# TensorE's program in a loop of two rounds, the first of which only jumps past it

## The chip, the core and the metric

The kernel runs on one core of one Trainium2 chip. The core has five engines with instruction streams of their own: TensorE (PE, matmuls; PEld is its loading of weights), VectorE (DVE), ScalarE (ACT), GpSimd (POOL) and SyncE (SP, which here only issues transfers), and 16 DMA engines that share the work of all DMA queues. The metric is the device time of one execution in microseconds (us).

## What is computed

One decoding step: one row `x` of 512 values, 32 heads, 8192 cached keys and values of 128 for each head, then a gate from a small GLU. All numbers are float32.

```python
def _A_ref(x, k_cache, v_cache, wq, wo):        # H, Dh = 32, 128; k_cache, v_cache: (1, 32, 8192, 128)
    q = (x @ wq).reshape(B, Sq, H, Dh).transpose(0, 2, 1, 3)
    scores = einsum("bhqd,bhkd->bhqk", q, k_cache) * (Dh ** -0.5)
    p = softmax(scores, axis=-1)
    o = einsum("bhqk,bhkd->bhqd", p, v_cache)
    return o.transpose(0, 2, 1, 3).reshape(B, Sq, H * Dh) @ wo

def _B_ref(x, w_gate, w_up, w_down):            # F = 1376
    return (sigmoid(x @ w_gate) * (x @ w_up)) @ w_down

xn = layernorm(x)
out = x + _A_ref(xn, ...) * silu(_B_ref(xn, ...))
```

Keys and values are 268 MB of the 294 MB that are read.

## The kernel before

All synchronisation is written out by hand with semaphores; nothing is scheduled by a planner. Each engine runs its own list of instructions in the order in which the program text calls that engine.

Heads are taken in 16 pairs (`NP`). One pair's keys are 8 MB, laid out as 128 partitions of 16384 numbers: head 2i in the upper 64 partitions, head 2i+1 in the lower. There are three such buffers: `slots[0]` and `slots[1]` take the keys by turns, `slots[2]` the values (and before them `wq`, after them the weights of the GLU). The last pair's values go to `slots[0]`, and `wo` to `slots[1]`.

*Prologue.* SP issues the loads of `wq` and of the first two pairs' keys; ACT those of `x`. Layer norm follows on DVE, PE and ACT (L179-L198), then q = xn @ wq on PE (L206) and its spreading over the partitions (L218).

*Pairs.* For pair i, DVE multiplies the keys by q (L281) and sums over the 128 numbers of each key (L282), which gives the scores; L284 takes their maximum per partition. PE turns these maxima into a row (L246), DVE reduces the row to two numbers (L276), PE spreads them (L248), ACT forms the exponentials (L296), PE sums them (L250). When the pair's values are there, 32 matmul lines weigh them (L255), ACT copies the sums (L301), PE gathers them (L260), DVE divides (L288, L289) and ACT places the result by two small transfers.

*Loads.* SP issues, one behind the other, the keys of pair i, when pair i-2's sums have been taken (L282), and the values of pair i-1, when L255 of pair i-2 has ended and so left `slots[2]` (L312-L314). Its queue is in order: a wait for the one holds up the other.

*TensorE's program.* All engines but PE have their pairs unrolled. PE's first 15 pairs are a loop (L265), since its instructions are the same for each; waits inside it are by `taken` (L240), which waits for a semaphore and takes the counted value away again. `head_slot={PE.engine: 0}` has the loop's first instruction loaded at the first slot of an instruction-fetch block, so padding stands ahead of it. The last pair stands behind the loop (L269), since its values are in another buffer; then come the matmuls of the GLU (L356, L384), the folds (L377) and those with `wo` (L402, L406). In PE's stream each matmul line of the program, in float32, is two weight loads and two matmuls.

Of the kernel before, what the change touches and what calls it, by code (L numbers as in the profile page):

```python
# [12 lines left out]

P = 128
EPS = 1e-5


@with_exitstack
def kernel(
# [12 lines left out]
    nc = tc.nc  # L32
# [6 lines left out]
    NP = H // 2  # L39
# [17 lines left out]

    W_ENDS, W_FOLD = (14, 24, 28, 30, 31, 32), 28

    PE, DVE, ACT, SP, POOL = nc.tensor, nc.vector, nc.scalar, nc.sync, nc.gpsimd  # L60

# [5 lines left out]
    def sb(name, *shape):  # L69
        return nc.alloc_sbuf_tensor(name, [P, *shape], F32)[:]  # L70
# [10 lines left out]
    slots = [sb(f"slot{i}", SLOT) for i in range(3)]  # L81
# [27 lines left out]
    def semaphore(name):  # L109
        sems.append(nc.alloc_semaphore(name))  # L110
        return sems[-1]


    class Steps:
        def __init__(self, name):
            self.sem, self.n = semaphore(name), 0
# [9 lines left out]
    def load(eng, name, dst, src, *after):  # L126
        wait(eng, *after)
        if name not in loads:
            loads[name] = [semaphore(f"s_{name}"), 0]
        loads[name][1] += 16  # L130
        eng.dma_start(dst, src).then_inc(loads[name][0], 16)  # L131
        return loads[name][0], loads[name][1]

    def wait(eng, *steps):
        for s in steps:
            if s is not None:
                eng.wait_ge(*s)
# [4 lines left out]
    s_val = semaphore("s_val")  # L142
# [27 lines left out]
    ld_xr = load(ACT, "xr", x_row[0:P:GP, :], xv.rearrange("(g c) -> g c", g=NG), c_xrow)  # L170
    c_eps = dve(DVE.memset(eps_t, EPS))
    c_id = pool(POOL.memset(ident, 0.0))
# [29 lines left out]
    for k in range(KT):  # L202
        for b in range(NQ // NG):
            for g in range(NG):
                c = (b * NG + g) * QT
                ins = PE.matmul(big[b][g * GP:g * GP + 1, :], xn[:, k:k + 1], wq_t[:, k, c:c + QT],  # L206
                                start=(k == 0), stop=(k == KT - 1))
# [32 lines left out]
    def taken(sem, n):  # L240
        PE.wait_ge(sem, n)
        PE.nop().then_inc(sem, -n)  # L242

    def pair(v, loaded):
        taken(maxed, 1)
        PE.matmul(pt[0:1, :], mx[:, 0:1], ident, start=True, stop=True).then_inc(turned, 1)  # L246
        taken(reduced, 1)
        PE.matmul(pm, ones[:1, :], mx[:1, 1:3], start=True, stop=True).then_inc(spread_m, 1)  # L248
        taken(powers, 2)
        PE.matmul(pn[:, Dh:], half, rs, start=True, stop=True)  # L250
        loaded()

        for j in range(0, NB, HT):
            g = j // HT % NG
            ins = PE.matmul(po[g * GP:g * GP + 2 * HT, :], weights[:, j // HT, :], v[:, j * Dh:(j + HT) * Dh],  # L255
                            start=(j < HT * NG), stop=(j >= NB - HT * NG))
        ins.then_inc(valued, 1)
        taken(copied, 1)
        for b in range(HT):
            ins = PE.matmul(pn[:, :Dh], pick[:, b:2 * HT:HT], o1[:, b * Dh:(b + 1) * Dh],  # L260
                            start=(b == 0), stop=(b == HT - 1))
        ins.then_inc(picked, 1)

    wait(PE, c_pick, c_id)
    with nc.Fori(0, NP - 1, engines=OrderedEngineSet([PE.engine]), head_slot={PE.engine: 0}):  # L265
        pair(slots[2], lambda: taken(s_val, 16))

    v_last = semaphore("s_v_last")
    pair(slots[NP % 2], lambda: PE.wait_ge(v_last, 16))  # L269


    summed, outs, placed = {}, {}, {}
# [78 lines left out]
    for dst, src, ld in ((big[0], wg_t, ld_g), (big[1], wu_t, ld_u)):  # L351
        wait(PE, ld)
        for c0, f0, w, g1 in ((0, 0, FW, 0), (FW, F - P, GP, g0)):
            for k in range(KT):
                for g in range(g1, NG):
                    ins = PE.matmul(dst[g * GP:g * GP + 1, c0:c0 + w], xn[:, k:k + 1],  # L356
                                    src[:, k, f0 + g * w:f0 + (g + 1) * w], start=(k == 0), stop=(k == KT - 1))
# [24 lines left out]
    for c in range(FP + 1):  # L382
        g = c % NG * GP
        ins = PE.matmul(big[0][g:g + 1, :], hid[:, c, 0:1], wd_t[:, c, :] if c < FP else wd_last,  # L384
                        start=(c < NG), stop=(c + NG > FP))
# [11 lines left out]
    for ld, r1 in zip(ld_o, W_ENDS):  # L397
        wait(PE, ld)
        for r in range(r0, r1):
            if r < W_FOLD:  # L400
                g = r % NG * GP
                ins = PE.matmul(big[0][g:g + 1, :], o_all[:, r:r + 1], wo_t[:, r, :],  # L402
                                start=(r < NG), stop=(r + NG >= W_FOLD))
                continue
            for g in range(NG):
                ins = PE.matmul(acc[g * GP:g * GP + 1, :], o_all[:, r:r + 1], wo_t[:, r, g * GC:(g + 1) * GC],  # L406
                                start=(r == W_FOLD), stop=(r == WR - 1))
# [8 lines left out]
    t = dve(DVE.tensor_mul(g_row, g_row, acc))  # L416
    wait(DVE, t)
    t = dve(DVE.tensor_add(g_row, g_row, x_row))  # L418
    SP.wait_ge(s_out, 16)
    SP.nop().then_inc(s_out, -16)  # L420
    wait(SP, t)
# [36 lines left out]
```

## Time and profile before

| | |
|---|---|
| time, median of 3 runs (lowest to highest) | 687.58 us (687.45 to 687.75) |
| profiled execution: span from its first to its last instruction | 685.6 us |
| instructions in the profile | 3694 |
| read from memory | 293.74 MB, 428 GB/s over the span |
| mean granted TensorE clock | 0.664 |

The profile is of one execution, and gives its span but no other time of it. Its page has, among other parts, the busy time of each engine; the span in 40 equal slices with a digit for the busy tenths of each; the DMA queues with packets, megabytes and the share of 16 engines' span that their packets took; and the chain of work that ended last, followed back from the last instruction. Queue q1 is SP's, q10 ACT's; queues of the kind "instruction" carry the engines' own programs. A timeline row is: start, duration, engine, line, operation, out<-in, partitions x elements, count, and in brackets the idle time before it and what ended that. "PEq" is PE's sequencer, which works through waits and jumps.

### The profile page before, as it was taken

The page shows a single profiled execution, that of the slowest core. Times are in us where ns is not written, and L with a number is a line of the kernel's source. Part 1 is how long each engine was busy: PE and PEld are TensorE (multiplying, and loading weights), DVE is VectorE, ACT ScalarE, POOL GpSimd, SP SyncE. Part 2 cuts the span into 40 slices and gives each one's busy share as a digit, 9 for nine tenths or more (in the row PEclk, how much of TensorE's full clock was granted, in tenths as well). Part 3 has the DMA queues.
Part 4 walks back from the last instruction along what each step waited for, and adds up shares of the span by engine and source line. Part 5 has one row for each costly group of instructions (what it writes and reads, how often), then busy time and mean ns, then how long its engine had stood idle before and what let it go on. Part 6 is the DMA issues. An engine that isn't in the chain of part 4 may idle for free.

```text
span 685.6 us, 3694 instructions
## 1 busy us (share of the span) xinstructions
PE 222.1 (32%) x1570; PEld 62.7 (9%) x1570; DVE 574.0 (84%) x136; ACT 40.9 (6%) x122; POOL 0.7 (0%) x6
## 2 busy tenths in 40 slices
PE   0550230605041140505042140506042140605656
PEld 0110000101010010101001010101000010101121
DVE  0159999999999999989898989989898989989220
ACT  0040100000000000000001010000001010000010
POOL 0000000000000000000000000000000000000000
PEclk9965575757566575757557575756657575756798
DMA  9999999999999999999999999999999999999996
GB/s 375 440 445 451 428 428 428 432 428 428 428 436 444 448 440 428 428 428 436 428 428 428 440 444 451 428 432 428 432 432 428 428 440 436 451 436 428 405 434 285
DMA packets 6614, 293.84 MB, mean 429 GB/s; under 512 B 1096, under 2 KB 1104, under 8 KB 1616
## 3 DMA queue, kind: packets, MB, share of 16 engines
q1 hardware_dynamic: 6200, 293.74, 99.1%
q10 hardware_dynamic: 408, 0.02, 0.0%
q8 instruction: 4, 0.07, 0.0%
q14 instruction: 2, 0.02, 0.0%
HBM read 293.74 MB, written 0.00 MB: 428 GB/s over the span
## 4 chain that ended last, share of the span: by engine, by line
DMA 37%; DVE 30%; PE 0%; SPq 0%; issue 0%
DMA slot<-in_A_k_cache_dram 31%; DVE slot L281 15%; DVE sc L282 15%; DMA slot<-in_A_wo_dram 6%; PE acc L406 0%; SPq L131 0%; PE pt L246 0%; PE acc L377 0%; DVE g_row L416 0%; DVE g_row L418 0%; DVE mx L276 0%
## 5 line engine op out<-in xcount | busy, mean ns | idle before, releaser
L281 DVE TENSOR_TENSOR slot<-slot,q_all 128x16384 f32<-128x16384 f32 x16 | 275.5, 17217 | 38.8 <-DMA slot<-in_A_k_cache_dram 38.8
L282 DVE TENSOR_REDUCE sc<-slot 128x128 f32<-128x16384 f32 x16 | 275.5, 17220 | 0.6
L255 PE MATMUL po<-slot,weights 128*8 128x512 f32 x1024 | 146.7, 737 | 232.1 <-PEq L242 231.5
L255 PEld LDWEIGHTS po<-slot,weights 128*8 128x8 f32 x1024 | 30.3, 103 | 335.3 <-issue 334.6
L246 PE MATMUL pt<-ident,mx 128*1 128x128 f32 x32 | 8.8, 374 | 148.6 <-PEq L242 148.6
L301 ACT COPY o<-po 128x512 f32<-128x512 f32 x16 | 9.4, 586 | 385.2 <-PE po L255 385.2
L260 PE MATMUL pn<-o,pick 128*2 128x128 f32 x128 | 16.5, 272 | 12.8 <-PEq L242 12.8
L180 DVE TENSOR_REDUCE st<-x_col 128x1 f32<-128x4 f32 x1 | 0.2, 157 | 20.7 <-DMA x_col<-in_A_x_dram 20.7
L246 PEld LDWEIGHTS pt<-ident,mx 128*1 128x1 f32 x32 | 1.8, 80 | 154.1 <-issue 154.1
L288 DVE RECIPROCAL rl<-pn 2x1 f32<-2x1 f32 x16 | 2.3, 146 | 14.6 <-PE pn L260 14.6
L294 ACT ACTIVATE nb<-pm 128x2 f32<-128x2 f32 x16 | 2.8, 173 | 190.4 <-PE pm L248 190.4
L416 DVE TENSOR_TENSOR g_row<-g_row,acc 128x128 f32<-128x128 f32 x1 | 0.3, 289 | 15.3 <-PE acc L406 15.3
L296 ACT ACTIVATE weights<-sc,nb 64x128 f32<-64x128 f32 x32 | 12.8, 399 | 0.9
L260 PEld LDWEIGHTS pn<-o,pick 128*2 128x2 f32 x128 | 9.9, 84 | 29.6 <-issue 27.2
L248 PE MATMUL pm<-mx,ones 1*128 1x2 f32 x32 | 8.8, 344 | 7.4 <-PEq L242 7.4
L402 PE MATMUL big<-slot,o_all 128*1 128x512 f32 x56 | 9.4, 765 | 4.8 <-DMA slot<-in_A_wo_dram 4.8
L250 PE MATMUL pn<-rs,half 128*2 128x1 f32 x32 | 3.0, 163 | 23.5 <-PEq L242 23.5
L218 PE MATMUL big<-q_all,ones 1*128 1x512 f32 x16 | 8.8, 850 | 1.6 <-ACT q_all L225 0.8
L206 PE MATMUL big<-slot,xn 128*1 128x512 f32 x64 | 9.0, 726 | 0.8 <-DVE xn L198 0.8
L248 PEld LDWEIGHTS pm<-mx,ones 1*128 1x128 f32 x32 | 7.9, 306 | 14.4 <-issue 14.4
L276 DVE TENSOR_REDUCE mx<-pt 1x2 f32<-1x128 f32 x16 | 4.5, 278 | 5.2 <-PE pt L246 5.0
L182 PE MATMUL pt<-st,ones 128*128 128x1 f32 x2 | 0.6, 362 | 23.4 <-DVE st L180 23.4
(61 smaller groups left out, 62.1 us busy)
## 6 DMA issues: line engine op xcount, KB each, us to landing
slot<-in_A_wo_dram SPq DMA_DIRECT2D x1, 3584.0 KB, 32.5
slot<-in_B_w_gate_dram SPq DMA_DIRECT2D x1, 2752.0 KB, 16.8
slot<-in_B_w_up_dram SPq DMA_DIRECT2D x1, 2752.0 KB, 22.8
slot<-in_B_w_down_dram SPq DMA_DIRECT2D x1, 2560.0 KB, 27.3
slot<-in_A_wo_dram SPq DMA_DIRECT2D x1, 2560.0 KB, 38.2
slot<-in_A_wo_dram SPq DMA_DIRECT2D x1, 1024.0 KB, 40.2
o_all<-on ACTq DMA_DIRECT2D x32, 0.5 KB
slot<-in_A_wo_dram SPq DMA_DIRECT2D x1, 512.0 KB, 40.9
```

The lines of the kernel that those rows point to most:

```text
L206: ins = PE.matmul(big[b][g * GP:g * GP + 1, :], xn[:, k:k + 1], wq_t[:, k, c:c + QT], start=(k == 0), stop=(k == KT - 1))
L218: spreads[t] = pe(PE.matmul(big[t % 2], ones[g * GP:g * GP + 1, :], q_row[g * GP:g * GP + 1, b, :], start=True, stop=True))
L246: PE.matmul(pt[0:1, :], mx[:, 0:1], ident, start=True, stop=True).then_inc(turned, 1)
L248: PE.matmul(pm, ones[:1, :], mx[:1, 1:3], start=True, stop=True).then_inc(spread_m, 1)
L255: ins = PE.matmul(po[g * GP:g * GP + 2 * HT, :], weights[:, j // HT, :], v[:, j * Dh:(j + HT) * Dh], start=(j < HT * NG), stop=(j >= NB - ...
L260: ins = PE.matmul(pn[:, :Dh], pick[:, b:2 * HT:HT], o1[:, b * Dh:(b + 1) * Dh], start=(b == 0), stop=(b == HT - 1))
L276: DVE.reduce_max(mx[:1, 1:3], pt[0:1, :].rearrange("o (e p) -> o e p", e=2), axis=AX.X).then_inc(reduced, 1)
L281: wait(DVE, dve(DVE.tensor_mul(k, k, qb[:, i:i + 1, :].to_broadcast([P, NB, Dh]))))
L282: summed[i] = dve(DVE.reduce_sum(sc[i % 2], k, axis=AX.X))
L296: ACT.activation(weights[h, :, e * HT:(e + 1) * HT], sc[i % 2][h].rearrange("p (g b) -> p g b", b=HT), AF.Exp, bias=nb[h, e:e + 1], scale= ...
L301: ACT.copy(o1, po).then_inc(copied, 1)
L402: ins = PE.matmul(big[0][g:g + 1, :], o_all[:, r:r + 1], wo_t[:, r, :], start=(r < NG), stop=(r + NG >= W_FOLD))
```

## The change

PE's calls are no longer made at once: `Later` stands in for the engine and notes each call with its arguments, and `play` makes them. The notes are taken in four parts: `before` (prologue), `each` (a pair in the loop), `last` (the last pair) and `after` (GLU and `wo`). At the end of the program they are played inside a new outer loop of two rounds, on PE alone: in round 0 the condition is false and PE jumps from the start of the program to the end of `last`, adds one to the counter and jumps back; in round 1 it runs `before`, the loop over 15 pairs, and `last`. `after` stands behind the outer loop. The inner loop has no `head_slot` any more.

PE's list has 999 instructions and labels in place of 991. The lists of the other engines keep their instructions and their order. In a profile of the changed kernel all matmuls carry the line of `play`.

```diff
+class Later:
+    def __init__(self, engine):
+        self.engine, self.notes = engine, []
+    def note(self, name, *args, **kwargs):
+        self.notes.append([name, args, kwargs, ()])
+        return Noted(self.notes[-1])
+    def __getattr__(self, name):
+        return lambda *args, **kwargs: self.note(name, *args, **kwargs)
+    def take(self):
+        notes, self.notes = self.notes, []
+        return notes
+    def play(self, notes):
+        for name, args, kwargs, inc in notes:
+            ins = getattr(self.engine, name)(*args, **kwargs)
+            if inc:
+                ins.then_inc(*inc)
+
+class Noted:
+    def __init__(self, note):
+        self.note = note
+    def then_inc(self, *inc):
+        self.note[3] = inc
...
-    PE, DVE, ACT, SP, POOL = nc.tensor, nc.vector, nc.scalar, nc.sync, nc.gpsimd
+    DVE, ACT, SP, POOL = nc.vector, nc.scalar, nc.sync, nc.gpsimd
+    PE = Later(nc.tensor)
+    pe_only = OrderedEngineSet([nc.tensor.engine])
...
     wait(PE, c_pick, c_id)
-    with nc.Fori(0, NP - 1, engines=OrderedEngineSet([PE.engine]), head_slot={PE.engine: 0}):
-        pair(slots[2], lambda: taken(s_val, 16))
+    before = PE.take()
+    pair(slots[2], lambda: taken(s_val, 16))
+    each = PE.take()
 
     v_last = semaphore("s_v_last")
     pair(slots[NP % 2], lambda: PE.wait_ge(v_last, 16))
+    last = PE.take()
...
     t = dve(DVE.tensor_add(g_row, g_row, x_row))
+    after = PE.take()
+
+    with nc.Fori(0, 2, engines=pe_only) as visit:
+        with PE.engine.If(visit > 0):
+            PE.play(before)
+            with nc.Fori(0, NP - 1, engines=pe_only):
+                PE.play(each)
+            PE.play(last)
+    PE.play(after)
```

## The prediction, made before the changed kernel was run

> **What bounds the kernel now.** I read the page's busy shares first, then its DMA lines.
>
> ```profile
> PE 222.1 (32%) x1570; PEld 62.7 (9%) x1570; DVE 574.0 (84%) x136; ACT 40.9 (6%) x122; POOL 0.7 (0%) x6
> DMA  9999999999999999999999999999999999999996
> q1 hardware_dynamic: 6200, 293.74, 99.1%
> q8 instruction: 4, 0.07, 0.0%
> q14 instruction: 2, 0.02, 0.0%
> ```
>
> The 16 DMA engines work without a hole: the packets of q1, on which all caches and weights come, fill 99.1% of 16 engines' span, and VectorE, the busiest engine, only 84%. So the time is bytes over rate, and whatever an engine carries besides q1 lengthens it. The page says what else there is: q8 carried four packets of instructions, 0.07 MB (16 KB each), q14 two smaller ones. Next, one steady period in the chain of waits, and the end of that chain:
>
> ```profile
> 449.07 17.24 DVE slot L281
> 466.33 17.23 DVE sc L282
> 483.57 42.80 DMA slot<-in_A_k_cache_dram
> 526.40 17.24 DVE slot L281
> ...
> 639.57 40.94 DMA slot<-in_A_wo_dram
> 680.54 0.62 PE acc L406 x16
> ```
>
> The score multiply that starts at 526.40 waits for its keys, whose load took 42.80 us because others stood ahead of it; the last pieces of wo set the end at 680.5, and some 2 us of matmuls and two VectorE operations follow. TensorE, which alone is changed, hangs in this pipeline so (timeline around 480, cut):
>
> ```profile
> 478.34 0.33 SPq L161 DMA_DIRECT2D slot<-in_A_v_cache_dram  x1
> 479.08 1.03 PE L260 MATMUL pn<-o,pick 128*2 128x128 f32 x8 [0.80 <-PEq L242]
> ...
> 484.01 0.39 PE L246 MATMUL pt<-ident,mx 128*1 128x128 f32 x2 [3.90 <-PEq L242]
> 484.44 0.28 DVE L276 TENSOR_REDUCE mx<-pt 1x2 f32<-1x128 f32 x1
> ...
> 487.74 17.22 DVE L281 TENSOR_TENSOR slot<-slot,q_all 128x16384 f32<-128x16384 f32 x1 [3.02 <-DMA slot<-in_A_k_cache_dram]
> ...
> 507.20 5.33 PE L255 MATMUL po<-slot,weights 128*8 128x512 f32 x28 [20.20 <-PEq L242]
> ```
>
> A pair ends on TensorE at 480.11 (479.08 + 1.03). There stands the loop's jump back; TensorE then idles 3.90 us until the next maximum, and 20.20 us more for values. VectorE waits 3.02 us for keys after its part.
>
> **When instructions are fetched.** I asked the DMA view for short stretches: 0 to 48, 50 to 640, then 48.7 to 48.75, 49.6 to 49.75, 50.8 to 50.9, 647 to 647.5, 661.3 to 661.5 and 681.4 to 681.6. A packet counts where it starts, and its share is its time over 16 times the stretch.
>
> ```profile
> q1 hardware_dynamic: 336, 19.92, 97.3%
> q10 hardware_dynamic: 152, 0.00, 0.2%
> ...
> q1 hardware_dynamic: 4384, 255.85, 100.1%
> q10 hardware_dynamic: 224, 0.01, 0.0%
> q14 instruction: 2, 0.02, 0.0%
> ...
> q8 instruction: 1, 0.02, 120.0%
> ...
> q1 hardware_dynamic: 1, 0.07, 120.2%
> ...
> q1 hardware_dynamic: 1, 0.07, 151.2%
> ...
> q8 instruction: 1, 0.02, 11.8%
> ...
> q8 instruction: 1, 0.02, 27.5%
> ...
> q8 instruction: 1, 0.02, 32.1%
> ```
>
> No q8 packet until 48.7, one there, none in the 590 us of the loop. So q8 is TensorE's: one refill as it enters the loop at its block's start, nothing while it circles inside that block, three more behind it, one in each of the last stretches (647.3, 661.4 and 681.5, as the next view's bounds). [...] Its price: 1.200 x 16 x 0.05 = 0.96 us of one DMA engine; the one 64 KB packet in the next stretch took 1.202 x 16 x 0.15 = 2.88 us, where a common one (third stretch) takes 1.512 x 16 x 0.1 = 2.42. I put the packet at 49.6 on the same engine, since it starts as the refill ends: together 0.96 + 0.46 = 1.42 us of that engine for each refill.
>
> **The change part by part.** What a block holds, from the windows view (PE and PEld counts) of the prologue and between the last three refills:
>
> ```profile
> 0.00:46.00 46.00, 19.00 (x84) 5.30 (x84) 7.96 (x23) 7.39 (x17) 0.70 (x6) 0.94 0.96 410
> 647.26:661.41 14.15, 11.00 (x164) 4.19 (x156) 1.90 (x9) 2.33 (x3) 0.00 (x0) 0.97 1.00 427
> 661.41:681.52 20.11, 13.54 (x118) 2.90 (x118) 1.71 (x11) 1.45 (x3) 0.00 (x0) 0.83 0.94 397
> ```
>
> 320 and 236 matmuls and weight loads lie between refills, on average 278; the sequencer runs ahead of TensorE, so each alone is blurred. The prologue has 168 of them. The loop's body has 39 matmul lines, each twice a matmul and a weight load: 156, and some 7 instructions to wait and jump. Before, the body starts at a block's first slot and fits in. After, it follows the prologue directly, from about 180 to 343 of the program: the block's end falls inside it. [...]
>
> 1. *The first round*: a compare, a jump behind the last pair, an addition, a jump back. It costs up to four refills (there and the block behind, back and the block behind). It lies ahead of this row, TensorE's first matmul:
>
> ```profile
> 23.36 0.59 PE L182 MATMUL pt<-st,ones 128*128 128x1 f32 x2 [23.36 <-DVE st L180]
> ```
>
> 23.36 us of idle time hide it; bounds: nothing (refills before the loads start) and 4 x 1.42 us over 16 engines, 0.4 us. I count it as four refills.
>
> 2. *The unaligned loop.* Each round now passes the boundary and asks for the third block; if TensorE's instruction memory holds two blocks, that replaces the first, which the jump back needs again. So two refills a round, or three if the second block is fetched anew too; 14 jumps back make 28 or 42. With four from part 1, one at first passing and two in the last pair and behind: 35 or 49, against three before 680. Do they share the engines? This is the DMA share from 680 to 685 in 40 slices:
>
> ```profile
> DMA  6343322222105000000000000000000000000000
> ```
>
> All load engines end within 1.4 us. Three refills on one engine would leave it 4.3 us behind; so successive refills go to different engines, and I take turns. 35/16 and 49/16 mean two to four on the slowest engine, before one: with 3 and 4, (3 - 1) x 1.42 = 2.8 and (4 - 1) x 1.42 = 4.3 us. I take the middle, **+3.4 us**, being unable to choose between two and three refills a round. Lower end 14 refills in all, one more on the slowest engine: +1.4. Upper end uneven turns, five or six on one engine: +6 or so.
>
> 3. *The stall.* The jump back must wait for its block: the refill at 48.7 started 3.0 us after the prologue's last matmul (37.96 + 7.74 = 45.70):
>
> ```profile
> 37.96 7.74 PE L218 MATMUL big<-q_all,ones 1*128 1x512 f32 x12 [0.84 <-ACT q_all L225]
> ...
> 444.92 0.33 SPq L131 DMA_DIRECT2D slot<-in_A_k_cache_dram  x1
> ```
>
> 3.0 + 0.96 = 4.0 us, at worst two common packets and the refill, 5.8. From 480.11 that is 484.1 to 485.9, where L246 starts at 484.01: 0.1 to 1.9 us late, and VectorE's 3.02 us wait for keys takes it. I cost it at nothing. Values are freed by L255, 20 us later, when the next block is long there. And were L255 late, the next transfer of values stands behind the keys issued at 444.92 (second row), which land at 487.7, 9.4 us after 478.34. Without that cover each us late would cost a us for each pair.
>
> 4. *The tail* loses two or three refills from the busy end: its worth is within part 2. Recording TensorE's calls moves nothing on other engines or queues.
>
> [...]
>
> The page gives no time of the profiled execution but its span, 685.6 us; the 2.0 us to the median of the runs shown (687.58) I carry over: 687.58 + 3.4 = **691.0 us**.
>
> **The rivals.**
> - *All blocks stay.* Then the first round loads blocks 3 and 4 in the idle start, the boundary costs nothing, and two or three refills vanish from the stream. For it: every refill seen is the first of its block. [...] Price: the slices above show two tenths of 16 engines, some three, busy to 681.25, so freeing one engine wins little: 0 to 1.4 us, I take 0.4: 687.2, not slower. [...]
> - *The stall decides.* Place: the jump back at 480.11. L246 must start by about 487.0 for L276 to end (0.7 us on) by 487.74; so from a stall of 6.9 us VectorE's wait is used up. With two refills in series, some 10 us, 3.1 us a pair over the nine or so pairs where VectorE waits for keys: +28, 719. Against: the 20 us in which the second block can come. Near it: all refills on one engine, 35 x 1.42 = 50 us, against which the slices speak.
> [...]
> - *Faster by more than 1.4 us*: only if the fetches or the tail cost what I can't see; about 686.
>
> **How the numbers follow.** Forecast (two blocks held, stall hidden) 0.57; stall or one engine 0.07; all blocks stay 0.28; boundary missed 0.04; faster 0.04. A change of 0.2%, 1.4 us, is about what a measurement here can tell. Slower 0.57 + 0.07 = 0.64, same 0.28 + 0.04 = 0.32, faster 0.04. The forecast's own range is 689.0 to 694.0; holding 8 in 10 needs the second case, so the range is 687.0 to 694.0.
>
> **What would show it.** Right: q8 with 35 to 50 packets, two or three in each pair of 38.6 us, the first before 10 us; L246 no more than 2 us late against the maximum (the 3.90 us idle shrinks to none), VectorE's wait for keys still above zero; DMA at 9 throughout and wo landing some 3 us later. Wrong: q8 with about five packets and none in the loop (all blocks stay, or the boundary missed), or VectorE's wait gone and holes in the DMA slices (the stall).

## The result, and the profile after

| | before | changed |
|---|---|---|
| median of 6 runs each (lowest to highest) | 687.52 us (687.36 to 687.75) | 689.39 us (688.87 to 690.56) |
| ratio of the times, 95% interval | | 1.0029 [1.0019, 1.0039] |
| profiled execution: its time, its span | not given, 685.6 us | 688.91 us, 687.1 us |

The change makes the kernel slower by 1.9 us, or 0.29%; "no change" lies outside the interval. The forecast was 691.0 us, so its direction held and its size was near twice too large. As the traces below show, its main cause was wrong. The profiled execution shows 1.5 us of the loss (687.1 - 685.6).

First the page of the changed kernel: busy shares, DMA slices, and the queues' packets.

```profile
PE 225.4 (33%) x1570; PEld 62.4 (9%) x1570; DVE 574.1 (84%) x136; ACT 40.9 (6%) x122; POOL 0.7 (0%) x6
DMA  8999999999999999999999999999999999999996
q1 hardware_dynamic: 6200, 293.74, 99.0%
q8 instruction: 7, 0.11, 0.1%
```

The matmuls, the work of the other engines and the bytes loaded are the same in number; of TensorE's instructions for loops and jumps eight more are in the profile (3702 instructions, before 3694). Queue q8 has seven packets in place of four; the forecast asked for 35 to 50. Where they are, the DMA view says for the stretches 0 to 24, 88 to 89 and 100 to 640 us:

```profile
q8 instruction: 3, 0.05, 1.2%
...
q8 instruction: 1, 0.02, 5.8%
...
q1 hardware_dynamic: 4030, 234.75, 100.3%
q10 hardware_dynamic: 224, 0.01, 0.0%
q14 instruction: 2, 0.02, 0.0%
```

Three refills in the first 24 us, one in the first pair, none in the other rounds of the loop (three more stand behind it, as before). So the unaligned loop asks for nothing, and what is new is at the start. Next the timeline there: TensorE's first matmul, the first product of scores, and the issue of the third pair's keys; below them the last two in the kernel before, where the first matmul came at 23.36.

```profile
26.13 0.59 PE L37 MATMUL pt<-st,ones 128*128 128x1 f32 x2 [26.13 <-DVE st L214]
...
45.05 17.23 DVE L317 TENSOR_TENSOR slot<-slot,q_all 128x16384 f32<-128x16384 f32 x1 [13.92 <-DMA slot<-in_A_k_cache_dram]
...
79.55 0.33 SPq L165 DMA_DIRECT2D slot<-in_A_k_cache_dram  x1
```

```profile
42.28 17.23 DVE L281 TENSOR_TENSOR slot<-slot,q_all 128x16384 f32<-128x16384 f32 x1 [13.93 <-DMA slot<-in_A_k_cache_dram]
...
76.79 0.33 SPq L131 DMA_DIRECT2D slot<-in_A_k_cache_dram  x1
```

All three are 2.8 us late, and the bracket of the second names the cause: it waits for the first keys. Finally the end of the chain of waits, with the last matmuls of the kernel before below:

```profile
646.05 37.27 DMA slot<-in_A_wo_dram
683.36 0.44 PE acc L37 x8
```

```profile
681.82 0.44 PE acc L406 x8
```

The last piece of wo lands at 683.32 and its matmuls start 0.04 us behind it. Before, they started at 681.82, behind a last landing of 681.77 (next table); the 680.5 at which the prediction's chain leaves wo is the landing of an earlier piece. So wo is 1.55 us later, which is the loss of the profiled execution.

The landings of single loads tell more. The trace has 16 records of a load's semaphore going up by one (for keys 0 before, from 41.57 to 42.26 us); I take each for the landing of one DMA engine's share. This table, worked out from those records of the profiled executions, gives the first and the last of the 16, in us. (The records don't name the engine: "the first engine" is the one that lands first.) "Values 0" stand ahead of "keys 2" (the third pair's) in the queue; "issued" is when SyncE issued the latter.

```
                      keys 0          values 0        keys 2    keys 2           last piece of wo
                      first  last     first  last     issued    first   last     first   last
before                41.57  42.26    80.25  81.95     76.79     99.63  101.26   680.02  681.77
changed               41.76  45.02    80.40  83.72     79.55    100.66  103.05   681.04  683.32
```

Keys 0 come on time on the first engine, but 2.8 us late on the last. From then on two things can be read off. The slowest engine stays some 2 us behind its place before: 45.02, 83.72 and 103.05 against 42.26, 81.95 and 101.26. And keys 2 take 100.66 - 80.40 = 20.26 us after values 0 on the first engine, where they took 19.38: a hole of 0.9 us on an engine that wasn't late at all. The first engine lost least: on the average of the 16 it is 20.34 against 19.32, 1.0 us.

### The profile page after: what moved, and what is told of

It reads as the page before. It is cut to its first block, busy times and chain, and to the rows that moved or that the text cites. A ratio compares the mean times of both kernels' runs of the same rounds, so it can differ in the third digit from the quotient of the medians.

```text
span 687.1 us, 3702 instructions
## 1 busy us (share of the span) xinstructions
PE 225.4 (33%) x1570; PEld 62.4 (9%) x1570; DVE 574.1 (84%) x136; ACT 40.9 (6%) x122; POOL 0.7 (0%) x6
## 4 chain that ended last, share of the span: by engine, by line
DMA 36%; DVE 30%; SPq 1%; PE 0%; issue 0%
DMA slot<-in_A_k_cache_dram 30%; DVE slot L317 15%; DVE sc L318 15%; DMA slot<-in_A_wo_dram 5%; SPq L165 1%; PE pt L37 0%; PE acc L37 0%; DVE g_row L452 0%; DVE g_row L454 0%; DVE mx L312 0%
## 5 line engine op out<-in xcount | busy, mean ns | idle before, releaser
L37 PE MATMUL po<-slot,weights 128*8 128x512 f32 x1024 | 148.4, 745 | 227.3 <-PEq L37 226.6
L37 PE MATMUL big<-slot,xn 128*1 128x512 f32 (+2 forms) x176 | 14.3, 482 | 1.5 <-DVE xn L232 0.8
L452 DVE TENSOR_TENSOR g_row<-g_row,acc 128x128 f32<-128x128 f32 x1 | 0.3, 288 | 14.1 <-PE acc L37 14.1
L37 PE MATMUL big<-q_all,ones 1*128 1x512 f32 (+1 forms) x24 | 10.1, 765 | 2.4 <-ACT q_all L259 0.8
```

What stands on the lines that cost most here:

```text
L37: ins = getattr(self.engine, name)(*args, **kwargs)
```

## The experiments

Times are medians, each against the kernel before on the same chip (687.48 to 687.53). The landings, again worked out from the semaphore records, stand here for all of them. The last column is the time from values 0 to keys 2 on the average of the 16 engines, 19.32 before and 20.34 in the changed kernel: what it has above 19.4 or so is the hole. (Where keys 2 are loaded in two halves, "1/2" marks the issue of the first.)

```
                            keys 0  values 0        keys 2    keys 2           last piece of wo   values 0
                            last    first  last     issued    first   last     first   last       to keys 2
e1_unaligned_alone          42.18   80.26  80.86     76.71     99.59  101.38   679.87  681.63     19.42
e2_two_rounds_aligned       45.23   80.38  83.83     79.76    100.97  103.14   681.51  683.65     20.42
e3_near_jump                43.45   80.37  82.36     77.98    100.34  102.42   680.78  683.31     20.54
e5_late_start               42.21   80.48  82.11     76.94     99.82  101.42   680.13  681.72     19.35
e6_linger                   43.30   80.28  81.92     77.84    100.26  103.09   680.48  683.20     20.38
e7_late_scores              42.21   80.27  82.14     80.87    102.04  102.52   682.95  684.64     21.72
e8_quiet_start              48.19   85.22  86.80     82.72    104.98  107.01   685.35  688.26     20.23
e9_after_split              45.05   80.32  83.66  71.05 (1/2)  99.71  102.98   680.06  683.14     19.44
e10_near_jump_split         43.62   80.81  82.68  69.62 (1/2) 100.28  102.25   680.50  682.39     19.48
e11_before_split            42.27   80.42  82.16  68.26 (1/2)  99.79  101.48   679.99  681.75     19.36
e12_linger_split            43.36   80.34  81.96  69.36 (1/2)  99.72  101.55   679.98  681.73     19.44
```

### The two halves of the change

The kernel before without the alignment:

```diff
-    with nc.Fori(0, NP - 1, engines=OrderedEngineSet([PE.engine]), head_slot={PE.engine: 0}):
+    with nc.Fori(0, NP - 1, engines=OrderedEngineSet([PE.engine])):
```

> The kernel before with its pair loop no longer aligned, and no outer loop. Theory 1 (the first round costs, through its three refills among the first loads: 1.4, 2.9 and 3.0 us of three DMA engines): the unaligned loop is free, since at least three blocks are held; q8 has four packets, one of them in the first pair, at about 85 us in place of 48.7, and none in the later pairs; 687.5 us, within 0.3 us of the kernel before. Theory 2 (the unaligned loop costs): most of the 1.9 us is here, 689 us or more, with TensorE late behind a jump back.

687.58 us, ratio 1.0002 [0.9993, 1.0011]. The DMA view for 0 to 84, 84 to 90 and 90 to 640 us:

```profile
q1 hardware_dynamic: 608, 35.65, 98.8%
q10 hardware_dynamic: 152, 0.00, 0.1%
...
q8 instruction: 1, 0.02, 1.0%
...
q1 hardware_dynamic: 4087, 238.49, 100.0%
q10 hardware_dynamic: 224, 0.01, 0.0%
q14 instruction: 2, 0.02, 0.0%
```

The refill has moved from the loop's entry (48.7) into the first pair (85), as it would if the next block began in the middle of the body; that it does is my reading of the place. The 14 jumps back then ask for nothing: the stretch from 90 to 640 us has no packet on q8. (The span holds three refills, not four as expected: the one near its end is missing.) The unaligned loop is free.

The changed kernel with the alignment put back:

```diff
-            with nc.Fori(0, NP - 1, engines=pe_only):
+            with nc.Fori(0, NP - 1, engines=pe_only, head_slot={PE.engine.engine: 0}):
```

> The changed kernel with the pair loop aligned as before. Theory 1: q8 again has three packets before 13 us, one of them 0.9 us long and two near 2 us; first matmul at 25 to 26 us in place of 23.4; 689 to 690 us. Theory 2: back to 687.5 us.

689.77 us, 1.0035 [1.0022, 1.0049], with three refills before 24 us. The loss is all in the two rounds.

### A first round that jumps less far

The last pair behind the outer loop, so that the jump ends in front of it:

```diff
-            PE.play(last)
+    PE.play(last)
     PE.play(after)
```

> The changed kernel with the last pair taken out of the outer loop, so that the first round jumps only to the end of the pair loop, which by the count of instructions lies in the program's second block. Theory 1, if a jump inside the blocks held is free: one packet on q8 in the first microseconds (the third block), none when the first pair passes the boundary, three behind the loop: four in all, one engine 1.4 us late, 687.5 us, within 0.4. If any first round costs, whatever its target: three packets at the start and 689 us.

689.11 us, 1.0024 [1.0013, 1.0034]: up to the loop's end the packets came as the first case has it (of the three behind it, two lie in the span), but the time as the second. The DMA view for 0 to 20 and 20 to 640 us, then the first product:

```profile
q8 instruction: 1, 0.02, 0.3%
...
q1 hardware_dynamic: 4608, 268.44, 100.1%
q10 hardware_dynamic: 267, 0.02, 0.0%
q14 instruction: 2, 0.02, 0.0%
...
43.48 17.23 DVE L317 TENSOR_TENSOR slot<-slot,q_all 128x16384 f32<-128x16384 f32 x1 [13.95 <-DMA slot<-in_A_k_cache_dram]
```

Up to 640 us this kernel has one refill, as the kernels of before and of e1, and nothing paired; and yet it lost 1.6 us. What differs in its refills is the place of the first: at 5 us, ahead of keys 0, instead of 48.7 or 85, behind them. Keys 0 end 1.2 us late on one engine, keys 2 are issued 1.2 us late, and the table has a hole again: 100.34 - 80.37 = 19.97 us on the first engine, 20.54 on the average, 1.2 us more than before. So the number of refills doesn't explain the time, but what they delay.

### Late without a refill

Two kernels made something late with VectorE's memsets alone, starting from the kernel before. The first delays the prologue:

```diff
     wait(DVE, ld_x)
+    for _ in range(3):
+        wait(DVE, c_big[-1])
+        c_big = [dve(DVE.memset(t, 0.0)) for t in big]
```

> The kernel before with six memsets of 0.49 us on VectorE between the arrival of x and its sum: the prologue 2.9 us later, without any refill. Theory 1a (the slowest DMA engine sets the end, and a late start only makes the early engines wait): a hole in the DMA slices near 80 us on the engines that are early, the same end: 687.5 us, up to 0.3 more. Theory 3 (the late start itself costs, since the keys of the third pair are issued at 79.6 in place of 76.8 us and the queue runs dry): 688.5 us or more.

687.78 us, 1.0004 [0.9995, 1.0013]. This kernel missed its aim: the prologue was 3.4 us late, but q was ready 0.2 us behind keys 0 (the product starts at 42.43, the keys had landed at 42.21), so keys 2 were issued at 76.94, and no hole came. It shows that TensorE's late first matmul in the changed kernel is harmless. The second delays the first product itself:

```diff
         wait(DVE, ld_k[i], copies[i // 2])
+        for _ in range(16 if i == 0 else 0):
+            wait(DVE, dve(DVE.memset(sc[1], 0.0)))
```

> The kernel before with 16 small memsets on VectorE between the landing of the first keys and their multiplication, some 3 us in all, and no other refill than before. Theory 1a (in the changed kernel a refill makes one DMA engine's share of the first keys late, so VectorE starts its first product 2.8 us late, frees the first buffer late, and the keys of the third pair are issued too late to keep the queue filled near 80 us): the first product at about 45 us, the third keys issued at 79.5 to 80, a hole of about 1 us in the DMA slices at 80 to 82, every later landing about 1 us later: 688.4 us, 688.0 to 689.0. Theory 1b (only the late engines' own lag costs): 687.6 us.

690.27 us, 1.004 [1.0027, 1.0054]. Its timeline, and the DMA slices from 78.5 to 83.5 us (eight to the us), with those of the kernel before below:

```profile
46.37 17.23 DVE L283 TENSOR_TENSOR slot<-slot,q_all 128x16384 f32<-128x16384 f32 x1
...
80.87 0.33 SPq L131 DMA_DIRECT2D slot<-in_A_k_cache_dram  x1
...
DMA  0000090000000000000000000099999000000000
q1 hardware_dynamic: 33, 1.11, 64.7%
```

```profile
DMA  0000090000099999900000009000009999990000
q1 hardware_dynamic: 48, 2.10, 97.0%
```

A slice here counts the packets that start in it. Before, the engines start packets every 2.4 us: at 80 and again at 82.5. In e7 nothing starts between 79.3 and 81.7, though values 0 have landed on the first engine at 80.27: the queue is dry. The memsets took 4.0 us instead of 3, so the loss lies above the range expected (102.04 - 99.63 = 2.4 us on the first engine, and as much on the average), but the mechanism is as forecast, without any new refill: keys 2 issued late let the queue run dry, and nothing behind made that good (wo is 2.9 us late, 682.95 against 680.02).

### Holding the loads back

The changed kernel, whose first loads wait until TensorE is back:

```diff
+    back = semaphore("s_back")
+    PE.nop().then_inc(back, 1)
+    SP.wait_ge(back, 1)
+    ACT.wait_ge(back, 1)
     ld_wq = load(SP, "wq", ...)
```

> The changed kernel with the first loads held back until TensorE is back from its first round: the same refills, but with idle DMA engines. All theories: the time grows by what the loads are held back, 3 to 6 us. Theory 1: the refills take 0.6 to 0.9 us each and leave no lag, so the first keys land on all engines within 0.8 us, VectorE starts on time behind them, there is no hole 80 us after the first load, and the time less the delay of the first load is 687.0 to 687.8 us. If instead the two rounds cost TensorE time anywhere else, the time less the delay stays near 689 us.

694.0 us, 1.0089 [1.0076, 1.0103]. The first load went out at 5.84 instead of 0.96 us, and 694.0 - 4.88 = 689.1: no better than the changed kernel, and the number expected if the two rounds cost TensorE time elsewhere. But the start wasn't quiet. The DMA view from 5 to 8 us:

```profile
q1 hardware_dynamic: 15, 0.98, 95.9%
q8 instruction: 2, 0.03, 8.2%
```

Two refills, 8.2% x 16 x 3 / 2 = 1.97 us each, began at 5.54 and 6.13 and ran on beside the first packets of the loads (from 6.86), though TensorE had already passed its first instruction at 5.84; the one before them, alone at 2.17, took 1.15. Keys 0 were late on two engines once more (47.87 and 48.19, the first at 46.55). So the run can't price the pair on idle engines, and it can't exclude a cost of the two rounds elsewhere (e12 below does); it shows that the refills of the way back end after TensorE is back.

### Lingering at the target

```diff
+    linger = semaphore("s_linger")
+    for _ in range(8):
+        wait(DVE, c_big[-1])
+        c_big = [dve(DVE.memset(t, 0.0)) for t in big]
+    wait(DVE, c_big[-1])
+    DVE.nop().then_inc(linger, 1)
     wait(DVE, ld_x)
...
             PE.play(last)
+        with PE.engine.If(visit < 1):
+            nc.tensor.wait_ge(linger, 1)
+            nc.tensor.nop()
```

> The changed kernel whose first round stays about 8 us at the jump's target before it goes back (it waits there for a signal from VectorE). What it tells apart is which blocks are held. If a jump out of the blocks held drops them all, and the block behind the target was not seen in the changed kernel only because TensorE left at once: two refills before 10 us, two more after the way back, one in the first pair near 90 us, three behind the loop. If blocks once fetched stay: no refill near 90 us, and fewer behind the loop. Time 689 to 692 us either way.

689.36 us, 1.0027 [1.0017, 1.0037]. One refill came before 10 us, not two, then one by one two more after the way back, one in the first pair, and three behind the loop (the last after the span's end). So no second refill came while TensorE waited at the target, and the refills of the first round spared none later. In this kernel no refill overlaps another, and the lag of the slowest engine up to 82 us is that of the kernel before (81.92); but the hole is there, 100.26 - 80.28 = 19.98 us, and 20.38 on the average. The engine that ends keys 2 last (103.09) isn't one of the three of the first round: by the packets' times it took the hole, a first packet of 3.68 us instead of 2.42, and then the first pair's refill at 86.75 with a packet of 2.92 behind it.

### Both causes taken away

To fill the hole, the first pair's sum is made in two halves, and keys 2 are loaded in two halves, the first of them when the first half is summed:

```diff
+        if i == 0:
+            first.append(dve(DVE.reduce_sum(sc[0][:, :NB // 2], k[:, :NB // 2, :], axis=AX.X)))
+            summed[i] = dve(DVE.reduce_sum(sc[0][:, NB // 2:], k[:, NB // 2:, :], axis=AX.X))
...
+            if i == 2:
+                load(SP, "k0", slots[0][:, :SLOT // 2], rows_of(k_cache, 2)[:, :SLOT // 2], first[0])
+                ld_k[2] = load(SP, "k0", slots[0][:, SLOT // 2:], rows_of(k_cache, 2)[:, SLOT // 2:], summed[0])
```

On the changed kernel:

> The changed kernel, but the first pair's sum over its keys is made in two halves, and the third pair's keys are loaded in two halves, the first of them issued when the first half is summed: some 8.6 us earlier, near 71 us in place of 79.6. So the queue can't run dry at 80 us. Theory 1c (two causes side by side: the hole near 80 us, which holds up the engines that are early, and the lag of 3 us that the two paired refills leave on two engines, which alone is enough to set the end): the early engines land about 1 us earlier than in the changed kernel, the last one as late as before: 688.6 to 689.4 us. Theory 1a (the hole is all): 687.6 to 688.1 us.

688.88 us, 1.0022 [1.0013, 1.0031]. The first engine has keys 2 at 99.71, as before the change (99.63), and its share of wo at 680.06 (680.02). The last still lands at 102.98 and 683.14. The hole is gone; the loss stays for the most part (1.4 us of 1.9; the intervals of both ratios overlap), on the slowest engines.

On the near jump, which had only the hole:

> The kernel with the near jump (one refill at 5.3 us, 689.1 us) with the same halves. There only one engine had a lag of 1.8 us, about that of the kernel before, and every engine had a hole of 0.7 to 1 us near 81 us. Theory 1c and 1a: 687.5 to 688.0 us, with the keys of the third pair landed at 99.7 to 101.4 us. If the hole does not matter: 689 us again.

687.77 us, 1.0003 [0.9994, 1.0012]: here the same edit takes back nearly everything. The landings bear this out only in part. Keys 2 come 19.48 us after values 0 on the average, so the hole is gone; but they land at 100.28 to 102.25, not at 99.7 to 101.4 as expected, since values 0 were some 0.4 us late already: the packets that start from 68 to 72 us took 2.53 us on the average instead of 2.42. The profiled execution is the slowest of this kernel's eleven (687.98); where that slowness came from stays open. On the kernel before:

> The control: the kernel before with the same halves. It has no hole near 80 us, so nothing is to be won: 687.5 us, within 0.3 us.

687.38 us, 1.0 [0.9991, 1.0009]: the edit by itself wins nothing. Then on the lingering kernel, which has the far jump and all its refills, but one by one:

> The changed kernel with both repairs: the first round stays 8 us at its target, so that its three refills (all of the block fetching of the far jump is kept) run one by one, 0.9 us each on engines of their own, and the third pair's keys come in two halves, the first issued some 8.6 us earlier. Theory 1c (paired refills' lag, and the hole): neither is left, 687.5 to 688.0 us. If the two rounds, the far jump or the number of refills cost by themselves: 689 us as with either repair alone.

687.55 us, 1.0003 [0.9994, 1.0013]. The whole first round stays, and the time is that of the kernel before. Its refills from 0 to 24 us, in the view that the changed kernel has above with 1.2%, with its DMA slices from 680 to 685 us, and then the same slices of the changed kernel and of e9:

```profile
q8 instruction: 3, 0.05, 0.7%
...
DMA  8664553431100000000000000000000000000002
```

```profile
DMA  9999999965545343433322000000060000000000
```

```profile
DMA  5555545342220111111000000000000000000000
```

The first fence is e12: three refills in 0.7% x 16 x 24 = 2.7 us, 0.9 each, and engines that end by 681.4. The second is the changed kernel: three in 4.6 us, and all engines are still at work to 681, the hole's doing; the digits 2 reach 682.7. The third is e9: like e12 it thins out from the first slice on, and a few engines, the digits 1, go on to 682.3.

No version was found that beats the kernel before.

## Why the prediction was right and wrong

- *What bounds the kernel* was right: DMA engines' work, to the end (q1 fills 99.0% of 16 engines' span in the changed kernel). Faster or slower was decided here by what else an engine carries (the refills; 1.4 us in e9) and by whether the queue is ever dry (2.8 us in e7).
- *Price of a refill*, 1.42 us of one engine, held for one alone: the first in the changed kernel took 0.88 us and the key packet behind it 2.96 instead of 2.42. It failed for the two that were requested together. The DMA view for 12.4 to 12.6, 14.0 to 14.1 and 14.55 to 14.65 us:

```profile
q8 instruction: 2, 0.03, 114.8%
...
q1 hardware_dynamic: 1, 0.07, 230.0%
...
q1 hardware_dynamic: 1, 0.07, 213.1%
```

  114.8% x 16 x 0.2 = 3.67 us for both, and the packets behind them 3.68 and 3.41 us: (3.67 + 1.26 + 0.99) / 2 = 3.0 us each, twice the price.
- *Turns among the engines*: held; by the landing records of keys 0 in the changed kernel three engines are late, at 43.38, 44.76 and 45.02, and the other thirteen done by 42.27.
- *Part 1, the first round*: **this step failed.** "23.36 us of idle time hide it" is true of TensorE (in e5 even 3.4 us more cost nothing that can be told from none) and beside the point. The refills delay a share of keys 0, and that delays VectorE's first product, the freeing of the first key buffer and the issue of keys 2. Besides, the two requested together leave 3 us of lag on two engines to the end. I priced the refills as work for 16 engines, 0 to 0.4 us, and not by what stands behind them in the queue. The first round was the whole loss, 1.9 us: with it alone the loss is there (e2), without it there is none (e1).
- *Part 2, the unaligned loop*, the whole of the forecast's +3.4 us: **this step failed too.** It rested on "if TensorE's instruction memory holds two blocks" and had 28 or 42 refills in the loop; there is one, in its first round (e1), and it costs nothing (687.58 us against 687.53). (The middle of 2.8 and 4.3 would be 3.55, besides, not 3.4.) No run shows a memory of two blocks, nor that each round asks for a third: no record names the block that a refill brings, and none says how many are held. In place of 28 or 42 refills the runs show none behind the first round, and in place of four for the outer loop's first round three. They show besides that a refill can end after TensorE has gone on: in e8 the two of the way back ended at 7.5 and 8.1, though TensorE had executed the first instruction behind it by 5.84.
- *All blocks stay*, the first rival, was half right: none in the loop after its first round, but the first round of the outer loop saved none later (seven packets, and the first pair asks for one as in e1). Whether the far jump drops blocks, and which the paired refills bring, the runs don't settle.
- *The stall* was costed at nothing. With no jump in the pair loop that asks for a refill it wasn't put to the test. The pair loop's jumps took 0.215 us (median of 15, L461; before 0.208, L265). The one long jump is that of the first round to its target: 6.34 us from 1.24 on (L459), with the refill from 5.20 to 6.07 in it. L246 starts in the changed kernel 0.43 us after the last maximum begins, which before took 484.01 - 483.58, the same (the pair that the prediction showed, in the timeline):

```profile
485.38 0.29 DVE L320 TENSOR_REDUCE mx<-sc 128x1 f32<-128x128 f32 x1
...
485.81 0.58 PE L37 MATMUL pt<-ident,mx 128*1 128x128 f32 x2 [4.83 <-PEq L37]
```

- *Range and size*: 689.39 lies within 687.0 to 694.0, the forecast of +3.4 us was too large by 1.5, and it came out on the right side for a reason that I had not given: a start that I had underpriced made up for a loop that I had overpriced. That the number is near is luck. The sign given for being wrong is what came: few packets on q8, and none in the loop behind its first round.

The two causes in the profiled executions: e9 without the hole keeps a last landing of 683.14, so the lag alone accounts for 1.4 of the 1.55 us (683.32 - 681.77) by which wo is late; e6 with a hole and no paired refills is 1.4 us late too. They don't add up, since they fall on different engines and the last one counts; of the kernels with the far jump only e12, without either, is back.

## What to carry to other kernels

A transfer that is off an engine's own path can be on that of the queue it shares: ask of each added packet what stands behind it on its DMA engine, and who waits for the last of the 16 (here three refills among the first loads, and VectorE, 2.8 us late at its first product). In a kernel that keeps the DMA queue full, look for the place where it is least full (here 80 us, where keys 2 were issued 3.5 us before the queue would have been empty, 76.79 against 80.25); what came later than that margin allowed wasn't made good behind it (e7: 2.4 us late at keys 2, 2.9 at wo). It isn't one for one: keys 2 issued 1.2 us later cost 1.2 us of the average engine (e3), 2.8 us later 1.0 (the changed kernel), 4.1 us later 2.4 (e7). A refill of instructions behind the first loads was free here (e1), among them it cost 1.6 us (e3).

## What was not expected of the hardware

- *A load issued one packet's time ahead of the queue's end was too late.* In e3 and e6 keys 2 were issued 2.4 us before values 0 ended on the first engine (77.98 and 77.84 against 80.37 and 80.28), and yet that engine lost 0.6 us and the average one 1.1 to 1.2; in e5 with 3.5 us (76.94 against 80.48) it lost nothing. One 64 KB packet took 2.42 us (before, at 50.8).
- *Two refills at once cost twice as much each* in the changed kernel: 3.0 us of an engine against 1.42 before. By themselves they took 1.64 and 2.04 us in the changed kernel, and 0.93 one by one in e6, the first of them at the same place (12.4 us).
- *The far jump brought refills when it went and when it returned* (one and two, e6), and the first pair asked for one more afterwards; the near jump brought one in all up to the loop's end (e3). Whether the target decides this isn't shown.
